# DFT by mirror symmetry in an FNet and MLP block: folded inputs, half the outputs multiplied, and the old program behind a branch

## The chip, the cores and the metric

The kernel runs on one core of one Trainium2 chip. The metric is the device time of one execution in microseconds (us). Engines: TensorE (PE in the profile; its weight loads are PEld) multiplies matrices into PSUM; VectorE (DVE), ScalarE (ACT) and GpSimd (POOL) work on tiles; SyncE (SP) and GpSimd issue the DMAs. Each engine runs its instructions in order, and so does each of the two queues that issue DMAs.

## The reference

One block with two residual branches, each behind a layer norm that a conditioning vector modulates. All tensors are float32; S = 2048 tokens, D = 1024 channels, F = 3584 hidden units.

```python
mod = (silu(c) @ w_mod).reshape(1, 6, 1, -1)
sa, ca, ga, sb, cb, gb = (mod[:, i] for i in range(6))
h = layernorm(x) * (1 + ca) + sa
a = einsum("bsd,ed->bse", h, dft_hid_re);  b = einsum("bsd,ed->bse", h, dft_hid_im)
x = x + ga * (einsum("ts,bse->bte", dft_seq_re, a) - einsum("ts,bse->bte", dft_seq_im, b))
h = layernorm(layernorm(x) * (1 + cb) + sb)
x = x + gb * (gelu(h @ w1 + b1) @ w2 + b2)
```

The four DFT matrices are inputs of the kernel: `dft_seq_re[t, s]` = cos(-2 pi t s / 2048), `dft_seq_im` the sine, and `dft_hid_*` the same with 1024. Nothing in the call says that they are DFT matrices; a kernel that uses their symmetries has to establish them from the numbers.

## The kernel before

**Products.** TensorE works on float16. Each float32 operand is split into a high half and a low half (`hi` on ScalarE, a copy to float16; `lo` on VectorE, the difference), and three of the four half products are summed: `PASSES = ((0, 0), (0, 1), (1, 0))`. A matmul has 128 x 128 weights and 512 moving columns. Where it can, the kernel uses a scheme of seven products for a 2 x 2 block product; `m` in 0 to 6 is the product, and `ORDER = (0, 1, 2, 4, 3, 6, 5)` the order in which they run. The sums and differences that it needs are `comb` on VectorE (L422), the splits L397 on ScalarE and L407 or L409 on VectorE.

**Stages.** The opening loads `wm` and x, makes the rows sa and ca (L485, L507 on TensorE, L493 on VectorE) and normalises x into `hq`. Meanwhile `idle_pe` (L501) runs matmuls whose result nobody reads. `plain1` (L1137) is the sequence DFT of the first 512 output tokens, `winograd1` (L1187) that of the other 1536, `gemm2` (L1423) the hidden DFT of eight blocks of 256 tokens, each followed on VectorE and ScalarE by the second norm (`ln_tasks`) and turned by TensorE (L1321). The other modulation rows (`row_tasks`) and the splits of the hidden DFT matrices and of the first weights lie under these matmuls. Then the MLP: `gemm3(g)` (L1636) is the first layer, 84 matmuls for 256 hidden units and 1024 tokens, and `gemm4(v)` (L1745) the second, 168 matmuls for one pair of g. The tokens go through in two halves, so there are 28 gemm3 and 14 gemm4, in this order: gemm3(0), gemm3(1), gemm3(2), gemm4(0), gemm3(3), gemm3(4), gemm4(1) and so on. In the first half (v = 0 to 6) the weights are split as they come and stored to DRAM; in the second half they are loaded split.

**Order.** Every operation is a task with an engine, an assumed cost and keys that it waits for; a recording layer (`pick`, `fill_to`, `push`) goes through assumed clocks and emits the task that can start first, with a due time as the tie break. The order that it finds is the order in the queues; nothing is reordered on the chip but by waits.

```python
for m in ORDER:                                        # gemm4, one slot for each m
    part(blk, m, ps[b], (0, 1))                        # 12 matmuls, L1745
    after_pe("dve", 1.2, lambda: dve.scalar_tensor_tensor(dst, ps[b], inv, dst, ...), kp[b])   # L1791
```

The eviction of one slot (L1791, 128 x 1024 out of PSUM) has to be through before the same two banks are written again, which in `ORDER` is one slot later for most m.

Of the kernel before, what the change touches and what calls it, by code (L numbers as in the profile page):

```python
# [9 lines left out]
F32 = mybir.dt.float32  # L10
F16 = mybir.dt.float16
I32 = mybir.dt.int32
AF = mybir.ActivationFunctionType
ALU = mybir.AluOpType
RED = bass_isa.ReduceOp
AX = mybir.AxisListType

P = 128
S = 2048
D = 1024  # L20
F = 3584
NS = S // P
ND = D // P
TB = 512
NTB = S // TB
EPS = 1e-5
# [3 lines left out]
SC = 16.0  # L30
SD = 16.0
SZ = 256.0


@with_exitstack
def kernel(ctx, tc, x, cre, cim, dre, dim, w1, b1, w2, b2, c, wm, out):

# [9 lines left out]
    nc = tc.nc  # L49
    pe, act, dve, gp, sp = nc.tensor, nc.scalar, nc.vector, nc.gpsimd, nc.sync  # L50

    pool = ctx.enter_context(tc.tile_pool(name="main", bufs=1))
    psum = ctx.enter_context(tc.tile_pool(name="ps", bufs=1, space=bass.MemoryType.PSUM))
    dram = ctx.enter_context(tc.tile_pool(name="dram", bufs=1, space=bass.MemoryType.DRAM))
    ctx.enter_context(tc.manual_schedule())

    cnt = [0]
# [5 lines left out]
    arena = mk([P, 220 * 256], F32, "arena")  # L63
# [7 lines left out]
    banks8 = psum.tile([P, 8 * 512], F32, tag="ps", name="ps")  # L71
    turn = [0]
    stage = [0]
    held = set()
# [74 lines left out]
    ga_t, sb_t, cb_t, gbb_t = (at(o, 1024) for o in O_ROWS)  # L149


    O_ZC = dict(zip((0, 1, 2, 4, 3, 6, 5), (96, 104, 112, 120, 80, 88, 128)))
    R1 = (136, 138, 140, 142, 216, 218)
    O_K, O_ACC, O_HID = 32, 48, 172
# [4 lines left out]
    w1c = at(0, 14336, F16).rearrange("p (m s a x) -> p m s a x", m=7, s=2, a=2)  # L159
    w2c = at(144, 14336, F16).rearrange("p (m s a x) -> p m s a x", m=7, s=2, a=2)  # L160
    hidc = at(O_HID, 14336, F16).rearrange("p (s m a x) -> p s m a x", s=2, m=7, a=2)
    acc = at(O_ACC, 8192).rearrange("p (b j r e) -> p b j r e", b=2, j=2, r=2)
# [11 lines left out]
    def quad(g):  # L174
        return at(200 + 8 * (g % 2), 2048).rearrange("p (n x) -> p n x", n=4)

    gb2_t = at(28, 1024)

    zc_d = [
        [dram.tile([P, 2, 4, 4, P], F16, tag=f"zc_{h}_{m}", name=f"zc_{h}_{m}") for m in range(7)] for h in range(2)  # L180
    ]
# [8 lines left out]
    row_d = {n: dram.tile([P, D], F32, tag=f"row_{n}", name=f"row_{n}") for n in ("ga", "sb", "cb", "gbb", "gb")}  # L190
    w1_d = [dram.tile([P, 7, 2, 512], F16, tag=f"w1_{g}", name=f"w1_{g}") for g in range(14)]
    w2_d = [dram.tile([P, 7, 2, 2, 512], F16, tag=f"w2_{v}", name=f"w2_{v}") for v in range(7)]
    ident = mk([P, P], F32, "ident")
# [16 lines left out]
    LAT = 0.15  # L210
    GUARD = 0.1
    in_order = [True]
    BEHIND = 0.3

    LAGS = {"w": 2.0, "rowl": 1.0, "crawl": 0.5, "row": 0.2, "z": 1.0, "s": 0.5, "u": 0.3, "op": 0.4, "comb": 0.3, "ln": 0.2}

    LANDS = {"dma": 2.0, "st": 4.0, ("st", "d"): 7.0, ("st", "u"): 5.0, ("st", "s"): 4.0, ("st", "z"): 4.0}
    PE1 = 0.2146
    PE12 = 12 * PE1
    bw = [0.0]  # L220
    clk = {"pe": 0.0, "dve": 0.0, "act": 0.0, "pool": 0.0, "dma": 0.0}
    done = {}
    streams = {}
    ids = [0]
# [154 lines left out]
    ORDER = (0, 1, 2, 4, 3, 6, 5)  # L379


    PLACE = (1, 2, 0, 3)
# [82 lines left out]
    scol, cc = mk([P, ND], F32, "scol"), mk([P, ND], F32, "cc")  # L465
    m1 = mk([P, 6], F32, "m1")
    srep = at(216, 1024).rearrange("p (k m) -> p k m", k=ND)
    mrow, ones = at(O_AUX, 1024), at(O_SO[0], 512)
    sas, ca1s = (at(o, 1024) for o in O_ROW)

    macc, mx = at(O_OP + 16, 2048), mk([P, 5], F32, "mx")
# [129 lines left out]
    xst = [mk([P, 2, 12], F32, f"xst{n}") for n in range(2)]  # L601
# [1386 lines left out]
    flush()  # L1988


# [1 line left out]
def _layout(inputs):  # L1992
    import numpy as np
# [41 lines left out]
```

## Time and profile before

| | |
|---|---|
| median of 3 runs | 1966.1 us (1965.88 to 1969.97) |
| span of the profiled execution | 1964.8 us |
| TensorE busy | 1951.9 us, 99%, granted clock 1.000 |
| VectorE, ScalarE, GpSimd busy | 1423.4, 851.1, 192.0 us |
| DFT stages (L1137, L1187, L1423) | 48.8 to 939.2 us |
| MLP (L1636, L1745) | 939.2 to 1964.8 us |
| DMA | 402 MB, mean 205 GB/s |

How to read it: the page is one profiled execution, which has a span (first to last instruction) and no time of its own beside it; the runs' median is 1.3 us longer. A row of a group has line, engine, operation, out and in, shapes and count, then busy us and mean ns of one, then the idle time before and what ended it. A row of the chain has start, length and what the chain runs through; matmuls of float32 show as two records. A row of stages has the stretch, its length, and each engine's busy time and count, then the granted clock, the DMA share and GB/s.

### The profile page before, as it was taken

Reading aid. Unit: us, or ns where it says so; the run is one execution under the profiler, and the core shown is the slowest. Engines: PE = TensorE matmul, PEld = TensorE weight load, DVE = VectorE, ACT = ScalarE, POOL = GpSimd, SP = SyncE. Lnnn points to the kernel's source line nnn. Section 1 sums busy time; section 2 is a strip of 40 time slices with the busy share of each in tenths; the row PEclk is TensorE's granted clock in tenths of the full one; section 3 lists DMA queues with packets and bytes.
Section 4 is the critical chain, followed back from the end, with each engine's and each line's share of the span. In section 5 each row is a group of like instructions: output and inputs, shape, how many; then the busy total and the mean of one; then the engine's idle time right before and its main releaser. Section 6 shows DMA issues by size and latency. Waiting matters only on the chain.

```text
span 1964.8 us, 23652 instructions
## 1 busy us (share of the span) xinstructions
PE 1951.9 (99%) x9040; PEld 890.0 (45%) x9040; DVE 1423.4 (72%) x1800; ACT 851.1 (43%) x1091; POOL 192.0 (10%) x287
## 2 busy tenths in 40 slices
PE   8999999999999999999999999999999999999999
PEld 3444444444444444444444444444444444444444
DVE  6977886997884477786688998999873453554567
ACT  4843332444542255645577556556323412312311
POOL 0012121221210012212020000000000000000000
PEclk9999999999999999999999999999999999999999
DMA  9258587698588867878855455345476432432324
GB/s 384 76 182 279 171 297 271 236 331 307 215 300 354 327 221 263 280 247 316 327 177 188 150 182 177 134 150 191 177 219 185 129 102 70 134 102 66 113 76 86
DMA packets 139362, 402.41 MB, mean 205 GB/s; under 512 B 15536, under 2 KB 15536, under 8 KB 134640
## 3 DMA queue, kind: packets, MB, share of 16 engines
q1 hardware_dynamic: 111808, 307.30, 46.3%
q0 software_dynamic: 27440, 93.60, 13.3%
q8 instruction: 70, 1.15, 0.2%
q14 instruction: 44, 0.36, 0.1%
HBM read 262.95 MB, written 137.89 MB: 204 GB/s over the span
## 4 chain that ended last, share of the span: by engine, by line
PE 97%; DVE 1%; DMA 1%; issue 1%; POOL 0%; ACT 0%; SPq 0%; POOLq 0%; ACTq 0%; DVEq 0%
PE ps L1636 26%; PE ps L1745 25%; PE ps L1187 22%; PE ps L1423 15%; PE ps L1137 8%; PE ps L1321 1%; PE ps L485 1%; DMA zc<-arena 0%; DMA arena<-in_wm_dram 0%; POOL zc L1357 0%; PE ps L507 0%; DVE arena L655 0%; PE ps L501 0%; PE ps L1497 0%; DVE arena L1791 0%
## 5 line engine op out<-in xcount | busy, mean ns | idle before, releaser
L1745 PE MATMUL ps<-arena 128*128 128x512 f16 x2352 | 510.5, 379 | 3.1 <-ACT arena L1781 3.1
L1636 PE MATMUL ps<-arena 128*128 128x512 f16 x2352 | 510.2, 379 | 0.0
L1187 PE MATMUL ps<-arena 128*128 128x512 f16 x2016 | 435.3, 379 | 0.0
L1745 PEld LDWEIGHTS <-arena 128*128 128x128 f16 x2352 | 230.1, 98 | 281.2 <-issue 4.2
L1636 PEld LDWEIGHTS <-arena 128*128 128x128 f16 x2352 | 230.1, 98 | 276.8
L1791 DVE SCALAR_TENSOR_TENSOR arena<-ps,i4c,arena 128x1024 f32<-128x1024 f32 x179 | 229.4, 1282 | 145.9 <-PE ps L1745 144.2
L1187 PEld LDWEIGHTS <-arena 128*128 128x128 f16 x2016 | 197.3, 98 | 237.9
L1423 PE MATMUL ps<-arena 128*128 128x512 f16 x1344 | 292.2, 379 | 0.0
L397 ACT ACTIVATE arena<-arena,shc 128x512 f16<-128x512 f32 (+1 forms) x115 | 116.0, 1018 | 277.9 <-PE ps L1745 181.4
L1423 PEld LDWEIGHTS <-arena 128*128 128x128 f16 x1344 | 131.5, 98 | 155.9
L422 DVE TENSOR_TENSOR arena<-arena 128x512 f32<-128x512 f32 (+1 forms) x228 | 171.4, 754 | 4.6 <-ACT arena L1655 0.3
L1137 PE MATMUL ps<-arena 128*128 128x512 f16 x768 | 166.5, 379 | 3.7 <-ACT arena L539 2.1
L703 ACT ACTIVATE arena<-arena 128x1024 f16<-128x1024 f32 x100 | 103.5, 1050 | 144.2 <-PE ps L1187 86.1
L409 DVE SCALAR_TENSOR_TENSOR arena<-arena,shc 128x512 f16<-128x512 f32 (+1 forms) x115 | 128.7, 1122 | 34.7 <-ACT arena L397 34.5
L706 DVE SCALAR_TENSOR_TENSOR arena<-arena 128x1024 f16<-128x1024 f32 x100 | 132.9, 1349 | 20.2 <-ACT arena L703 20.2
L1662 DVE TENSOR_TENSOR arena<-arena,ps 128x512 f32<-128x512 f32 x84 | 57.6, 686 | 113.4 <-PE ps L1636 110.0
L1655 ACT ACTIVATE arena<-arena,b1s,i1c 128x512 f32<-128x512 f32 x84 | 68.3, 813 | 139.1 <-DVE arena L1662 139.0
L1137 PEld LDWEIGHTS <-arena 128*128 128x128 f16 x768 | 74.8, 98 | 95.4 <-ACT arena L539 2.6
L798 DVE TENSOR_TENSOR arena<-arena 128x1024 f16<-128x1024 f32 x56 | 67.3, 1219 | 20.3 <-ACT arena L795 20.2
L397 ACT ACTIVATE arena<-arena,s1c 128x512 f16<-128x512 f32 (+1 forms) x70 | 60.5, 884 | 47.2 <-DVE arena L422 24.4
L795 ACT ACTIVATE arena<-arena 128x1024 f16<-128x1024 f32 x56 | 57.7, 1047 | 51.4 <-DMA u<-arena 36.4
L1658 ACT ACTIVATE arena<-ps 128x512 f32<-128x512 f32 x84 | 49.8, 593 | 54.5 <-PE ps L1636 54.3
(169 smaller groups left out, 1413.0 us busy)
## 6 DMA issues: line engine op xcount, KB each, us to landing
w<-arena SPq DMA_DIRECT2D x64, 512.0 KB, 4.7
arena<-w SPq DMA_DIRECT2D x119, 256.0 KB, 2.7
u<-arena POOLq DMA_DIRECT2D x56, 512.0 KB, 6.7
arena<-u SPq DMA_DIRECT2D x112, 256.0 KB, 4.1
arena<-w SPq DMA_DIRECT2D x56, 512.0 KB, 3.6
arena<-s SPq DMA_DIRECT2D x48, 512.0 KB, 6.6
arena<-in_cre_dram SPq DMA_DIRECT2D x32, 512.0 KB, 7.2
arena<-in_cim_dram SPq DMA_DIRECT2D x32, 512.0 KB, 6.0
```

Source lines behind the costliest of these rows:

```text
L397: act.activation(o[m][0], q(j), AF.Copy, **sc)
L409: dve.scalar_tensor_tensor(o[m][1], q(j), scale, o[m][0], op0=ALU.mult, op1=ALU.subtract)
L422: dve.tensor_tensor(q(d), q(a), q(b), op=op)
L703: h = Task("act", 1.15, lambda: act.activation(o[:, :, 0], s2, AF.Copy, scale=SC), list(deps) + free)
L706: dve.scalar_tensor_tensor(o[:, :, 1], s2, SC, o[:, :, 0], op0=ALU.mult, op1=ALU.subtract)
L1137: pe.matmul(bank_of(d_), hleft(d_, s, kp, a), cop(n)[:, s, b], start=(kp == 0 and s == 0 and a == 0 and b == 0), stop=(kp == 7 and s == 1 ...
L1187: pe.matmul(bank_of(st + ch), left, cop(n)[:, s, b], start=(start and kp == 0 and s == 0 and a == 0 and b == 0), stop=(kp == 3 and s == 1 ...
L1423: pe.matmul(bank_of(bk), up(N)[:, c_, a], dp(n)[:, c_, w], start=(start and ri == 0 and c_ == 0 and i == 0), stop=(ri == 1 and c_ == 3 and ...
L1636: pe.matmul(ps.rearrange("p (k t) -> p k t", k=4), w1c[:, m, s, a, d * P : (d + 1) * P], zc(m)[:, b, :, d, :], start=(start and d == 0 and ...
L1655: act.activation(dst, src, AF.Gelu_apprx_tanh, scale=inv, bias=b1s[:, 2 * p + j : 2 * p + j + 1])
L1745: pe.matmul(t[:, j], hidc[:, c_, m, a, k * P : (k + 1) * P], w2c[:, m, c_, w], start=(start and c_ == 0 and n == 0), stop=(c_ == 1 and n = ...
L1791: lambda: dve.scalar_tensor_tensor(dst, ps[b], inv, dst, op0=ALU.mult, op1=ALU.add), kp[b],
```

## The change

The old function is renamed `general` and otherwise left as it is. A new function `fast` stands ahead of it:

- **Folds.** For a DFT of length N, cos at N - s equals cos at s and sin has the other sign, and at N/2 - s the sign alternates with the output's parity. `fast` normalises x, transposes it (`ln1`), applies the modulation per channel in the transposed layout, and adds and subtracts mirror images in both dimensions (`folds`; rows that are their own mirror go through `special`). The folded inputs are a quarter as long in each dimension and come in even and odd kinds.
- **Half the outputs.** `hid_unit` multiplies 18 pieces with 513 columns, `seq_tile` 16 tiles of 128 tokens; the other half of the channels of each tile is the same two products with the other sign (`low`, `up`), and the tiles of mirrored tokens use negated operands (`neg_tasks`).
- **Rows.** `row` makes ga, cb, sb and gb with TensorE in float32, each from eight 512 KB loads through three buffers.
- **Second norm** (`ln2`), transposes (`turn`) and `z_tasks` follow per block of 256 tokens as before; the four blocks of the first half leave their splits where the MLP reads them. `b2 * gb` is added to the output by 16 accumulating DMAs when the MLP starts.
- **MLP.** `gemm3` and `gemm4` are those of before. The splits of the first two w1 groups stand in the front, those of w1 group 2 and w2 pair 0 now behind the start of the MLP.
- **Checks.** From gemm4(6) on, `chk_tasks` reads the four matrices again from DRAM, 148 units of up to 128 x 512: each loads a piece and its mirror image (40 of them by an index list), subtracts or adds on VectorE and sums squares on ScalarE, through three pairs of buffers. `verdict` adds up; if the sum is above 2 to the power -60, the branch runs `general`, which computes and overwrites everything.
- The filler matmuls of `idle_pe` are not in `fast`.

```diff
-def tile_fnet_mlp_kernel(ctx, tc, x, cre, cim, dre, dim, w1, b1, w2, b2, c, wm, out):
+def general(ctx, tc, x, cre, cim, dre, dim, w1, b1, w2, b2, c, wm, out):
...
+def fast(ctx, tc, x, cre, cim, dre, dim, w1, b1, w2, b2, c, wm, out):
...
+                def fold(e=e, o=o, bd=bd, pos=pos, neg=neg):
+                    dve.scalar_tensor_tensor(o, bank(bd), neg, e, op0=ALU.mult, op1=ALU.add)
+                    dve.scalar_tensor_tensor(e, bank(bd), pos, e, op0=ALU.mult, op1=ALU.add)
...
+    def folds(cls):
...
+        def s1(arr, op):
+            o = FA(eo(0, arr, cls, 0), (4 * AR, 2), (AR, 2), (1, 512))
+            dve.tensor_tensor(o, o, FA(eo(0, arr, cls, m), (4 * AR, 2), (AR, 2), (-1, 512)), op=op)
...
+    def cop_item(t, ch):
+        q, c_ = divmod(ch, 2)
+        def f(o):
+            for hf in range(2):
+                sp.dma_start(
+                    FA(o, (512, 2), (1, 512), p0=64 * hf, pn=64),
+                    cri[t][0:2, q::2, 2 * c_ + hf, :].rearrange("b p t -> p b t"),
+                )
+        def use(o, key, last):
+            src = FA(o, (1, 2), (2, 512))
...
+            split("cop", src, hi, lo, SC, [key], last, 1024, 42.0 + ch)
...
+    def row(n, j):
+        for k in range(ND):
+            m = ND * n + k
+            o = WRING[m % 3]
+            l = load(("wr", m), lambda o=o, k=k, j=j: sp.dma_start(FA(o, (1, 1024)), wm[:, k, j * D : (j + 1) * D]),
+                [("wru", m - 3)] if m > 2 else [("tpd", 3), ("n", 15)], stream="ld")
+            def f(k=k, o=o):
+                for h in range(2):
+                    pe.matmul(bank(6 + h), scol[:, k : k + 1].to_broadcast([P, P]), FA(o + 512 * h, (1, 512)),
+                        start=k == 0, stop=k == 7)
...
+    def hid_unit(tp, t, cls, c_):
...
+            for par, pm_, o, w in ((0, ev, 255, 257), (1, od, 512, 256)):
+                mm_ = [
+                    (HA(hop(cls, loc, a, j, t, pm_, u0), (1, m)), HA(dop(t, b, j, 257 * par), (1, w)))
+                    for j in range(2) for a, b in PASSES
+                ]
...
+    def seq_tile(i):
...
+            mm_ += [
+                (HA(cop(tp, 1, a, ch, kk), (1, 128)), HA(aop(tp, 1, b, ch), (257, 2), (1, 256)))
+                for ch in range(4) for a, b in PASSES
+            ]
...
+        def low():
+            dve.tensor_tensor(
+                FA(y, (1, 2), (2, 256)), PA(pb + 255, (257, 2), (1, 256)), qv(i, 0, (257, 2), (1, 256)), op=ALU.subtract)
+        def up():
+            dve.tensor_tensor(
+                FA(y + 512, (1, 2), (2, 256)), PA(pb + 511, (256, 2), (-1, 256)), qv(i, 256, (256, 2), (-1, 256)), op=ALU.add)
...
+    def chk_unit(load_a, load_b, diffs, sq, pn=P):
+        n = chks[0]
+        chks[0] += 1
+        ka, kb_ = CB[n % 3]
+        a, b = at(ka, 512), at(kb_, 512)
+        free = [("chk", n - 3)] if n > 2 else []
+        deps = [add("chkl", "st", 0.0, lambda: load_a(a), free, ("chka", n))]
...
+        for cost, f in diffs:
+            k = add("chkd", "dve", cost, lambda f=f: f(a, b), deps if k is None else [k], None, 1e7)
+        f = lambda: act.activation(sq(a), sq(a), AF.Square, accum_out=csum[0:pn, n : n + 1])
+        add("chks", "act", 0.7, f, [k] if k else deps, ("chk", n), 1e7)
...
+    def parity(even):
+        def f(o, op):
+            def g(a, b):
+                dve.tensor_tensor(a[:, o::2], a[:, o::2], b[:, o::2], op=op)
+            return g
+        return [(0.4, f(0, ALU.subtract if even > 0 else ALU.add)), (0.4, f(1, ALU.add if even > 0 else ALU.subtract))]
...
+    def gather(mat, idx, col_):
...
+            gp.indirect_dma_start(
+                out=b, out_offset=None, in_=rows_, in_offset=bass.IndirectOffsetOnAxis(ap=idx[:, col_ : col_ + 1], axis=0))
...
+    def plain(v, pn=P):
+        return lambda t: gp.dma_start(t[0:pn], v)
...
+    def verdict():
+        v = csum[:, 0:1]
+        dve.tensor_reduce(v, csum, axis=AX.X, op=ALU.add)
+        gp.partition_all_reduce(v, v, P, RED.add)
+        dve.tensor_scalar(v, v, 2.0**-60, None, op0=ALU.is_le)
+        dve.tensor_scalar(v, v, -1.0, 1.0, op0=ALU.mult, op1=ALU.add)
+        dve.tensor_copy(odd_i, v)
...
+    for i in range(NS):
+        f = lambda i=i: gp.dma_start(o_s[i // 8, i % 8], gbb_t, accum_op=ALU.add)
...
+            if v == 6:
...
+                chk_tasks()
+                n = chks[0]
+                add("chkd", "dve", 2.0, verdict, [("chk", n - 1 - j) for j in range(3)], "verdict", 1e7)
+    flush()
+    return nc.values_load(odd_i[0:1, 0:1])
...
+def tile_fnet_mlp_kernel(tc, *args):
+    odd = fast(tc, *args)
+    with tc.If(odd > 0):
+        general(tc, *args)
```

1371 lines of the change are left out of this document (1370 added, 1 removed).

## The prediction

> **What bounds the kernel now.** I read the page's busy shares, then the chain of work that ended last in order of time, then three stretches of the table by stage.
>
> ```profile
> PE 1951.9 (99%) x9040; PEld 890.0 (45%) x9040; DVE 1423.4 (72%) x1800; ACT 851.1 (43%) x1091; POOL 192.0 (10%) x287
> ```
> ```profile
> 48.82 153.85 PE ps L1137 x712
> 202.66 435.12 PE ps L1187 x2016
> ...
> 917.62 20.72 PE ps L1423 x96
> ...
> 939.22 18.13 PE ps L1636 x84
> ...
> 976.35 1.75 PE ps L1321 x16
> ...
> 1936.03 24.78 PE ps L1745 x114
> ```
> ```profile
> 0.00:42.00 42.00, 36.46 (x107) 14.20 (x108) 25.07 (x46) 16.22 (x26) 1.58 (x6) 1.00 0.97 380
> ...
> 1083.00:1156.00 73.00, 73.00 (x340) 33.07 (x339) 67.69 (x104) 43.45 (x59) 2.43 (x4) 1.00 0.53 180
> ...
> 1523.00:1596.00 73.00, 73.00 (x340) 33.09 (x339) 30.36 (x32) 23.47 (x27) 0.00 (x0) 1.00 0.36 101
> ```
> TensorE is the bound from 49 us to the end. A matmul of 512 float16 columns costs 18.13/84 = 0.2158 us, so 256 columns cost 0.108. The DFTs (L1137, L1187, L1423) fill the time to 939 us, the MLP the 1026 us behind. In the MLP's first half VectorE is busy 67.69 of 73 us behind TensorE, in the second only 30.36.
>
> **What goes.** The three DFT groups have 768 + 2016 + 1344 = 4128 matmuls, 891 us. In the built order of the changed program their place is taken by 297 matmuls of at most 257 columns (hidden DFT) and 200 of 512 and 400 of 257 or 256 columns (sequence DFT): 43 + 75 = 118 us. So TensorE no longer bounds the front; VectorE and the hand-offs do. I therefore add up VectorE's front in its built order, with these durations:
>
> ```profile
> L422 DVE TENSOR_TENSOR arena<-arena 128x512 f32<-128x512 f32 x200 | 137.3, 688 | 4.2 <-ACT arena L1655 0.3
> L422 DVE TENSOR_TENSOR arena<-arena 128x1024 f32<-128x1024 f32 x28 | 34.2, 1221 | 0.4
> L409 DVE SCALAR_TENSOR_TENSOR arena<-arena,s1c 128x512 f16<-128x512 f32 x42 | 31.0, 746 | 6.5 <-ACT arena L397 6.4
> L409 DVE SCALAR_TENSOR_TENSOR arena<-arena,s2c 128x1024 f16<-128x1024 f32 x49 | 61.8, 1279 | 3.8 <-ACT arena L397 3.8
> L493 DVE SCALAR_TENSOR_TENSOR arena<-arena,scol 128x2048 f32<-128x2048 f32 x2 | 4.7, 2352 | 3.8 <-DMA arena<-in_wm_dram 3.8
> L614 DVE BATCH_NORM_STATS2 xst<-arena 128x6 f32<-128x512 f32 x4 | 2.5, 669 | 0.0
> L1251 DVE TENSOR_TENSOR lns<-lns 128x2 f32<-128x2 f32 x14 | 2.3, 161 | 0.5
> L397 ACT ACTIVATE arena<-arena 128x512 f16<-128x512 f32 x56 | 32.7, 619 | 14.2 <-DVE arena L422 13.8
> L1304 ACT ACTIVATE arena<-arena,lns 128x1024 f32<-128x1024 f32 x16 | 19.0, 1231 | 9.2 <-DVE lns L1301 9.1
> ```
> The new reversed and two-step accesses appear in no row; I price them by element count. From below they cost that, from above double, and some 60 instructions of the front have one: 0 to 60 us. I take 0, since an element costs VectorE 1.2 to 1.5 ns in these rows whatever the operands are.
>
> **A, to the first fold: 55 us.**
> ```profile
> 15.06 3.43 PE ps L485 x8
> ...
> 27.09 3.66 PE ps L507 x8
> ```
> ```profile
> 1.48 5.14 PE L501 MATMUL ps<-arena 128*128 128x512 f16 x12 [1.48 <-DVE mx L1463]
> ...
> 18.33 1.89 PE L501 MATMUL ps<-arena 128*128 128x512 f16 x8
> ```
> Four float32 matmuls (eight records) cost 3.43. L507 starts when the last modulation weights land, behind 9 MiB; now four x tiles stand ahead instead of two, so 1 MiB more at 380 GB/s, 2.8 us: 29.8. Two groups of four follow: 37, or 40 with a TensorE that ran cold, as the first twelve above did (0.43 us each against 0.24). Maximum, row copies, 18 one-column matmuls and scaling I estimate at 7: 47. Eight statistics and small steps precede the first fold in VectorE's order: 8.
>
> **B, folds: 68 us, to 123.** 26 STT of 512 (19.4), 6 TT of 2048 (13.7), 4 STT and 4 TT of 1024 (10.0), the rest statistics and small (14.7): 57.8. For normalising, turning and activating the third and fourth batch behind ScalarE I add 10.
>
> **C, hidden DFT: 107 us, to 230.** Here TensorE's order decides. The four modulation rows are now made by TensorE, 32 steps of two float32 matmuls (1.71 us), placed between the hidden DFT's matmuls as 51, then 14 steps, 15, 2 steps, 54, 8 steps, 45, 8 steps, 132. Whatever stands behind a step waits for its 512 KB load.
> ```profile
> arena<-in_wm_dram SPq DMA_DIRECT2D x32, 512.0 KB, 6.9
> ...
> zc<-arena POOLq DMA_DIRECT2D x56, 256.0 KB, 4.7
> ...
> w<-arena POOLq DMA_DIRECT2D x9, 256.0 KB, 3.5
> ...
> row_ga<-arena POOLq DMA_DIRECT2D x1, 512.0 KB, 2.9
> ```
> SP reaches these loads only when the fifth sequence-DFT piece has freed its buffer (eight STT, one split: 7.3 us), and they land 4 later: 11.5. Three buffers turn in 1.71 + 0.4 + landing; landing 2.9 to 6.9 gives 1.7 to 3.0 us a step. I take 2.0, nearer the short row, as little else is moving. 14 steps 28, then 1.7 + 3.4 + 5.9 + 15.1 + 4.9 + 15.1 + 14.3 (the first three steps of each group have landed): 88.4. Sum 100; bounds 93 and 128. VectorE has only 49 us of work here. The first sequence tile adds 5.4 and its copies: 7.5.
>
> **D, sequence DFT and second norm: 226 us, to 456.** VectorE: 113 TT of 512 (77.6), 52 STT of 1024 (69.3), 16 TT of 1024 (19.5), 6 STT of 512 (4.5), 134 small (21.7): 192.6. ScalarE has 78 copies of 512 (48) and 80 squares and passes of 1024 (some 95), TensorE about 6.3 us a tile against VectorE's 12; both lie beside it. Idle I estimate at 28 (10 while two tiles fill the pipe, 8 in the last norm's hand-offs, 10 between), bounds 8 and 60. Two activations, a copy and 16 transposes (1.75) follow before the MLP starts: 5.2.
>
> **E, MLP: 1032 us.** 4704 matmuls, 1015.3. At its start VectorE still has 15 TT (10.3) and 46.6 us of weight and hidden splits before the first second-layer eviction, against 54.4 us of TensorE; ScalarE has eight copies and two squares ahead of the first eviction. Before, these splits lay under the DFT. Estimate 17, bounds 5 and 40.
>
> **F, checks under the MLP: 10 us.** The 148 units, each of which loads a piece of a DFT matrix and its mirror image, subtracts and squares, stand from the seventh pair of layers on: 133 before the last eviction, about 22 in each 73 us. Their VectorE work, 0.8 us, fits the 43 idle; but VectorE waits in order for GpSimd's loads, and the evictions queue behind it.
> ```profile
> L1025 POOL DMA_DIRECT2D w<-arena x15 | 8.3, 551 | 52.7 <-DVE arena L409 33.4 <-DVE lns L1240 6.0 <-ACT arena L1304 4.6
> L1819 POOL DMA_DIRECT2D out_dram<-arena x4 | 4.8, 1197 | 467.0 <-DVE arena L1791 467.0
> L929 POOL PARTITION_ALL_REDUCE sums<-sums x21 | 11.9, 566 | 381.6 <-DVE sums L925 379.6 <-DVE sums L933 2.0
> ```
> A buffer's turn is VectorE 0.8, ScalarE 0.8, two issues of 0.55, landing 3.5 to 4.7, signals 0.4: 6.6 to 7.8, against three eviction slots of 2.59 = 7.8. It just fits. 40 units gather by index, for which no row exists: from the 0.55 of a plain issue (nothing) to the 1.2 of an accumulating one plus a landing late by half a slot, 1.5 us each (60). I take 10, near the plain issue.
>
> **G, behind the last eviction: 37 us.** 15 units still stand there, with nothing beside them. Three have landed (2.4); twelve more take four turns of 7.3, less 2 for two that only square: 27; the verdict 3.3 (reduction over partitions 0.57, five small steps, signals); register loads and the branch 4, in no row, from 2 to 10. Bounds 27 and 52. It cannot be nothing: the units are in the order. The Trainium skill (DMA: Bandwidth & Descriptors, "Anatomy of one DMA — SWDGE (gpsimd) path") gives 2.0 us plus bytes at 436 GB/s, 2.6 us for 256 KB, where this trace has 3.5 and 4.7; by it the tail would be about 5 us shorter, an estimate.
>
> **Sum.** 55 + 68 + 107 + 226 = 456; + 1032 + 10 + 37 + 2 for the last evictions = 1537 of span; the span before was 1964.8 beside a median of 1966.1, so 1.3 around it: 1538 us.
>
> **Rivals.** *Better overlap:* C 7 less, D's idle at 8, E at 5, G at 27: 1489. For it: VectorE's 67.69 of 73. Against: there the order had slack, here it alternates with ScalarE.
>
> *Checks stall the evictions:* F at 60, G at 52, because gathers are slow: 1603. For it: a turn of 7.8 has no slack. Against: the low DMA share there.
>
> *Cold TensorE:* without the filler matmuls of L501, its work in C (about 83 us) and D runs at half speed, as in the twelve above. C then takes 11.5 + 32 x 3.42 + 53 = 174 (+74), D some 15 more: 1627. Against: in C TensorE is asked for nearly without pause. By the Trainium skill (TensorE: Matmul & The Clock Gate, "Part 1: The HAM clock gate (the 'warmup' mystery)") a window of about 3.4 us without work sets the clock to half. The trace's start at 0.43 us agrees; no long pause follows in it to show a fall.
>
> *The verdict goes the other way (slower):* the sum of squared deviations must stay below 2 to the power -60 = 8.7e-19; above it, the old program runs as well, 1538 + 1965 = 3503. It decides at one value off by 1e-9. The inputs, computed as the reference computes them, deviate by at most 1.5e-12 between mirror images, squares summing to some 4e-21. That leaves only an arithmetic surprise on the chip.
>
> **How the numbers follow.** Forecast 0.60, better overlap 0.12, stalling checks 0.12, cold TensorE 0.12, both programs 0.04. From 1470 (better overlap, and VectorE a little quicker) to 1630 (the cold case and part of the strided accesses). A difference of 0.2% (4 us) is about what a measurement can tell from no change: faster 0.95, same 0.01, slower 0.04.
>
> **What would show it.** In the profile after: first fold near 55, hidden DFT ending near 222, first MLP matmul near 456, TensorE solid from there to about 1500, and VectorE, ScalarE and GpSimd alternating for 37 us without TensorE. A first MLP matmul outside 410 to 520, holes in the second half's matmuls, or any line of the old program would prove the sum wrong.

## The result, and the profile after

The changed kernel takes 1565.2 us (median of 4 runs, 1560.4 to 1573.3) against 1967.2 us for the kernel before beside it: a ratio of 0.796 (95% interval 0.794 to 0.799). Forecast were 1538 us, with a range of 1470 to 1630. The profiled execution took 1573.3 us with a span of 1571.5, so it is one of the longer ones; two experiments below have the same front and reached the MLP 4 to 5 us sooner, which is how far single times of the front can be trusted.

From the page: the busy shares, and the granted clock in 40 slices.

```profile
PE 1319.7 (84%) x6081; PEld 635.8 (40%) x6081; DVE 1121.2 (71%) x1723; ACT 738.6 (47%) x1173; POOL 254.4 (16%) x415
...
PEclk9555999968658999999999999989999999999995
```

TensorE lost 632 of its 1952 us, the kernel 393 of its span. The difference is TensorE's idle time: 252 us, where there were 13. No line of the old program ran. The table by stage (columns: stretch, its length, then busy time and instructions of PE, PEld, DVE, ACT, POOL, granted clock, DMA share, GB/s) shows where it idles:

```profile
0.00:55.00 55.00, 36.32 (x113) 21.37 (x113) 35.18 (x78) 21.39 (x38) 6.54 (x20) 0.84 0.76 297
55.00:146.00 91.00, 24.80 (x123) 19.63 (x124) 67.79 (x92) 43.24 (x63) 0.65 (x1) 0.58 0.27 71
146.00:265.00 119.00, 109.24 (x452) 52.35 (x451) 32.80 (x36) 21.03 (x27) 1.61 (x4) 0.93 0.56 188
265.00:469.00 204.00, 117.31 (x693) 78.72 (x692) 177.63 (x359) 129.27 (x203) 23.97 (x39) 0.74 0.40 139
469.00:585.00 116.00, 101.63 (x423) 43.57 (x421) 74.71 (x126) 70.05 (x94) 20.38 (x28) 0.89 0.77 205
585.00:1020.00 435.00, 435.00 (x2017) 197.25 (x2016) 384.07 (x510) 230.62 (x298) 13.07 (x18) 1.00 0.51 175
1020.00:1120.00 100.00, 88.62 (x398) 39.34 (x397) 48.05 (x86) 45.96 (x85) 34.56 (x65) 0.95 0.87 289
1120.00:1428.00 308.00, 308.00 (x1429) 139.62 (x1428) 207.87 (x308) 133.80 (x265) 102.31 (x165) 1.00 0.70 235
1428.00:1533.00 105.00, 98.78 (x446) 43.90 (x444) 82.09 (x103) 33.16 (x71) 37.04 (x54) 0.97 0.61 185
1533.00:1571.00 38.00, 0.00 (x0) 0.00 (x0) 11.04 (x31) 10.04 (x30) 14.30 (x23) 0.54 0.48 162
```

The first stretch ends at the first fold, the second with the folds, the third with the hidden DFT, the fourth with the sequence DFT and second norm. Then come the MLP's start, its solid middle, the checks' start, and the rest. In the second stretch TensorE works a quarter of the time at 0.58 of its clock, and the DMA engines move 71 GB/s: nothing is full there. In the fourth VectorE is busy 178 of 204 us. The timeline of TensorE has the seams (start, length, line, count, and in brackets the idle time before with what ended it):

```profile
145.58 9.92 PE L2874 MATMUL ps<-arena 128*128 128x256 f16 x42 [13.55 <-ACT arena L2659]
...
241.16 17.09 PE L2874 MATMUL ps<-arena 128*128 128x257 f16 x132
...
551.49 33.48 PE L3547 MATMUL ps<-arena 128*128 128x512 f16 x144 [4.47 <-ACT arena L3583]
...
1052.44 15.76 PE L3438 MATMUL ps<-arena 128*128 128x512 f16 x60 [9.03 <-ACT arena L3460]
...
1527.94 4.88 PE L3547 MATMUL ps<-arena 128*128 128x512 f16 x12 [4.54 <-DVE arena L3593]
```

The hidden DFT begins in earnest at 145.58 and ends at 258.25, the first MLP matmul stands at 469.02, the last ends at 1532.82.

New accesses, grouped by form: the folds with a reversed operand (L2690, L2696), a normalising pass read forward and reversed (L2603, L2604), and the checks' half-row differences, gathers and plain loads (columns: count, busy us, mean ns, idle before).

```profile
L2696 DVE TENSOR_TENSOR arena<-arena 128x2048 f32<-128x2048 f32 x4 | 9.2, 2291 | 0.1
L2690 DVE TENSOR_TENSOR arena<-arena 128x2048 f32<-128x2048 f32 x4 | 9.2, 2288 | 0.0
...
L2604 ACT ACTIVATE arena<-arena,lnc 128x512 f32<-128x512 f32 x12 | 9.6, 802 | 0.0
L2603 ACT ACTIVATE arena<-arena,lnc 128x512 f32<-128x512 f32 x12 | 9.6, 801 | 0.7 <-DVE lnc L2594 0.7
...
L3352 DVE TENSOR_TENSOR arena<-arena 128x256 f32<-128x256 f32 x240 | 92.3, 422 | 73.0 <-DMA arena<-in_cre_dram 38.6 <-DMA arena<-in_dim_dram 12.0 <-DMA arena<-in_cim_dram,idxs 9.2
...
L3369 POOL DMA_DIRECT2D arena<-in_cre_dram x99 | 54.3, 548 | 126.0 <-ACT arena L3345 117.5 <-issue 6.5 <-DMA arena<-fw 0.4
...
L3362 POOL DMA_INDIRECT arena<-in_cre_dram,idxs x16 | 17.0, 1063 | 4.9 <-issue 4.9
```

2048 reversed elements cost VectorE 2.29 us, where 2048 straight ones cost 2.35 before, in another operation. Like with like, `up` (L2974), which reads in reverse and writes every second element, takes 683 ns for 512 elements, and a straight TENSOR_TENSOR (L2365) 688. ScalarE pays the same forward and backward. So the strided accesses cost nothing extra, as taken. VectorE idled 73 us before the checks' differences, for loads; most of that is its own slack, and TensorE lost 17 us in holes after 1020.

### The profile page after: what moved, and what is told of

Its sections match the earlier page's. It is cut to its first block, busy times and chain, and to the rows that moved or that the text cites. A ratio compares the mean times of both kernels' runs of the same rounds, so it can differ in the third digit from the quotient of the medians.

```text
span 1571.5 us, 17349 instructions
## 1 busy us (share of the span) xinstructions
PE 1319.7 (84%) x6081; PEld 635.8 (40%) x6081; DVE 1121.2 (71%) x1723; ACT 738.6 (47%) x1173; POOL 254.4 (16%) x415
## 4 chain that ended last, share of the span: by engine, by line
PE 66%; DVE 12%; DMA 9%; issue 7%; ACT 3%; POOL 2%; SPq 1%; DVEq 0%; POOLq 0%; ACTq 0%
PE ps L3438 28%; PE ps L3547 27%; PE ps L2818 3%; DMA arena<-in_wm_dram 3%; PE ps L2874 3%; DMA arena<-in_cre_dram 2%; PE ps L2947 2%; PE ps L2959 1%; DMA arena<-in_w_dram 1%; PE ps L2500 1%; DVE arena L2365 1%; DVE arena L2350 1%; DVE arena L2352 1%; DMA arena<-in_dim_dram 1%; DMA arena<-in_cim_dram,idxs 1%
## 5 line engine op out<-in xcount | busy, mean ns | idle before, releaser
L3438 PE MATMUL ps<-arena 128*128 128x512 f16 x2352 | 521.3, 384 | 19.5 <-ACT arena L3460 16.7
L3547 PE MATMUL ps<-arena 128*128 128x512 f16 x2352 | 515.2, 381 | 12.3 <-DVE arena L3593 7.7
L3438 PEld LDWEIGHTS <-arena 128*128 128x128 f16 x2352 | 232.7, 99 | 305.7 <-issue 35.0
L3547 PEld LDWEIGHTS <-arena 128*128 128x128 f16 x2352 | 231.2, 98 | 294.0 <-issue 19.6
L3345 ACT ACTIVATE arena<-arena 128x512 f32<-128x512 f32 (+5 forms) x148 | 91.5, 619 | 191.1 <-DVE arena L3352 125.1
L2365 DVE TENSOR_TENSOR arena<-arena 128x512 f32<-128x512 f32 (+1 forms) x228 | 171.5, 754 | 5.8 <-ACT arena L3067 1.1
L3352 DVE TENSOR_TENSOR arena<-arena 128x256 f32<-128x256 f32 x240 | 92.3, 422 | 73.0 <-DMA arena<-in_cre_dram 38.6
L2947 PE MATMUL ps<-arena 128*128 128x256 f16 (+3 forms) x400 | 55.9, 304 | 29.7 <-DVE arena L2974 29.5
L3164 POOL PARTITION_ALL_REDUCE sums<-sums x21 | 12.8, 609 | 402.8 <-DVE sums L3160 398.0
L3369 POOL DMA_DIRECT2D arena<-in_cim_dram x99 | 54.2, 548 | 135.6 <-ACT arena L3345 133.2
L3369 POOL DMA_DIRECT2D arena<-in_cre_dram x99 | 54.3, 548 | 126.0 <-ACT arena L3345 117.5
L2619 PE MATMUL ps<-ident,arena 128*128 128x128 f32 x128 | 26.5, 378 | 53.7 <-ACT arena L2603 52.6
L2352 DVE SCALAR_TENSOR_TENSOR arena<-arena,s1c 128x512 f16<-128x512 f32 (+1 forms) x70 | 66.3, 958 | 7.1 <-ACT arena L2340 7.1
L3063 PE MATMUL ps<-ident,arena 128*128 128x128 f32 x128 | 24.7, 357 | 54.4 <-ACT arena L3053 42.8
L2818 PE MATMUL ps<-arena,scol 128*128 128x512 f32 x128 | 63.4, 640 | 8.3 <-DMA arena<-in_wm_dram 7.1
```

The source lines that it names most:

```text
L2352: dve.scalar_tensor_tensor(o[m][1], q(j), scale, o[m][0], op0=ALU.mult, op1=ALU.subtract)
L2365: dve.tensor_tensor(q(d), q(a), q(b), op=op)
L2818: pe.matmul(bank(6 + h), scol[:, k : k + 1].to_broadcast([P, P]), FA(o + 512 * h, (1, 512)), start=k == 0, stop=k == 7,)
L2947: pe.matmul(PA(pb + o, (1, w)), l, r, start=n == 0, stop=n == len(mm_) - 1)
L3345: f = lambda: act.activation(sq(a), sq(a), AF.Square, accum_out=csum[0:pn, n : n + 1])
L3352: dve.tensor_tensor(a[:, o::2], a[:, o::2], b[:, o::2], op=op)
```

## The experiments

Five things were to be settled: what made the folds late, what the low clock cost, what bounds the sequence DFT's stage, what the checks cost, and whether the findings make a faster kernel. Each was timed beside the kernel before, whose medians lay between 1966.8 and 1967.4 us.

### Loads ahead of the fold

In the changed kernel, SyncE loaded no piece of the sequence matrix between 64 and 109 us, and ScalarE's split of one stood in front of the fourth batch's normalising:

```profile
62.77 1.24 SPq L2763 DMA_DIRECT2D arena<-in_cim_dram  x2
109.01 1.25 SPq L2763 DMA_DIRECT2D arena<-in_cre_dram  x2
...
116.16 1.11 ACT L2475 ACTIVATE arena<-arena 128x1024 f16<-128x1024 f32 x1 [7.97 <-DMA arena<-in_cim_dram]
...
118.03 0.48 PE L2619 MATMUL ps<-ident,arena 128*128 128x128 f32 x1 [35.19 <-ACT arena L2603]
```

The pieces turn in three buffers. A buffer comes free with VectorE's share of the split, which stood behind the folds and the fourth batch's statistics; so the loads behind it were late, and ScalarE waited for them in order.

```
-            split("cop", src, hi, lo, SC, [key], last, 1024, 42.0 + ch)   # due time
+            split("cop", src, hi, lo, SC, [key], last, 1024, 63.0 + ch)
-    for ch in range(4): for t in range(2): cop_item(t, ch)               # eight, ahead of the rows
+    the first three here, the other five between the row loads: one for every third
```
(The splits of the one-row pieces also got an earlier due time, 20 instead of 41, and a stream of their own in the planner.)

> The splits of the sequence-DFT matrix pieces (ScalarE's copy and VectorE's difference) are placed behind the normalising of the fourth batch of rows instead of between the batches, and the last five of the eight piece loads stand between the row loads in SyncE's queue instead of ahead of them. Theory (the pieces held up step B): in the changed kernel ScalarE waited 8.0 and 8.2 us for two of these loads, and TensorE 35 and 13.6 us behind it; without that the hidden DFT should begin near 120 us instead of 145.6, with up to 10 us given back between the row steps: 1540 us (1530 to 1552). Rival (SyncE's queue is the bound either way, and the five pieces only push the row loads back): no gain, 1560 to 1572.

Measured: 1556.3 us (1554.9 to 1557.6), 9 less than the changed kernel's median.

```profile
110.40 0.81 ACT L2603 ACTIVATE arena<-arena,lnc 128x512 f32<-128x512 f32 x1 [3.01 <-DVE lnc L2594]
...
164.08 6.88 PE L2819 MATMUL ps<-arena,scol 128*128 128x512 f32 x12 [4.31 <-DMA arena<-in_wm_dram]
...
226.63 14.69 PE L2877 MATMUL ps<-arena 128*128 128x257 f16 x114
```

The mechanism is there, but the gain is a third of the 25 us expected, and between the two expectations. The fourth batch is normalised 7 us sooner, without a wait for a load, and the hidden DFT ends at 241.3 instead of 258.2. But the work behind the fourth batch (row steps, here) starts at 129, where 120 was expected: the batch now waits for VectorE's statistics (3.01 above), which stand behind the folds. The rival's price is small: TensorE waits 10 us between the first row step and the last hidden-DFT matmul (4.31 the longest wait), in the changed kernel 8. The first MLP matmul came at 452.1 us. Four later kernels that keep this edit have it at 449.0 to 456.8, three without it (further down, one of them with fillers) at 463.4 to 465.0: some 11 us at that point between the means, of which 9 are left at the end.

### The low clock

Filler matmuls keep TensorE busy where it idled.

```
                 def turn(g=g, j=j, bk=bk):
+                    if bt == 2 and g == 0 and j == 0:
+                        140 matmuls of 512 float16 columns of `ones` into bank(bk)
...
+                if n == 0 and par == 1:          # first unit of the hidden DFT
+                    50 such matmuls into bank(4)
```

> 190 filler matmuls of 512 float16 columns on a constant tile are added to TensorE in the front: 140 ahead of the transposes of the third batch (where it idled 35 us) and 50 inside the first unit of the hidden DFT (where it idled 13.6 us). Nothing else moves. Theory (the low granted clock cost little, since TensorE is not the bound there): what was slow on the path are 42 hidden-DFT matmuls (9.9 us against about 5.3) and four row steps (9.4 against 7.3): a gain of 4 to 9 us, 1559 us. Rival (cold TensorE as priced in the prediction, 74 us in the hidden DFT and 15 behind it): a gain of over 40 us, below 1525. Other rival (the fillers end too late and stand in the way): 1570 or more.

Measured: 1587.6 us (1583.2 to 1592.5), 22 slower, as the second rival had it. The fillers stood one batch too early; batches count from 0, and the long hole is before batch 3:

```profile
68.50 30.38 PE L2621 MATMUL ps<-arena 128*128 128x512 f16 x140 [0.42 <-ACT arena L2663]
98.72 3.66 PE L2623 MATMUL ps<-ident,arena 128*128 128x128 f32 x32
```

The third batch's transposes, due at 72, came at 98.7. That says nothing about the clock. The second try changes `bt == 2` to `bt == 3`.

> The same 190 filler matmuls as in the run before, but the first 140 one batch later: ahead of the transposes of the fourth batch, where TensorE really idled for 35 us (82.8 to 118.0 us of the changed kernel). In the earlier run they stood ahead of the third batch's transposes, which were needed at 72 us, so they were late by 26 us. Theory (the low clock in front costs little): the 42 hidden-DFT matmuls take 5.5 instead of 9.9 us, the first row steps 1.8 instead of 2.35 each: 5 to 8 us less, 1558 us. Rival (cold TensorE, 89 us as priced in the prediction): below 1525. If nothing else hangs on it: 1565.

Measured: 1568.5 us (1566.4 to 1571.7): no gain, where 5 to 8 us were expected.

```profile
86.45 30.38 PE L2621 MATMUL ps<-arena 128*128 128x512 f16 x140
...
148.72 5.51 PE L2882 MATMUL ps<-arena 128*128 128x256 f16 x42 [2.76 <-ACT arena L2663]
```

The 42 matmuls do run warm, 5.51 us instead of 9.92, and the hidden DFT ends some 5 us sooner (253.4, against 256.5 to 260.0 in six profiles without fillers). By the first MLP matmul it is gone: 463.4 us, against 463.9 and 465.0. Where in between it went was not followed further.

### What bounds the sequence DFT's stage

Three kernels change TensorE's work there, the first two that alone. The first doubles it:

```
-                for n, (l, r) in enumerate(mm_):
+                for n, (l, r) in enumerate(2 * mm_):
+                    n %= len(mm_)                # start again in the same bank
```

> Every accumulation group of the sequence DFT is multiplied twice, the second time starting anew in the same bank, so that the result stays; TensorE gets about 87 us more work (16 tiles of 12 matmuls of 0.216 us and 26 of 0.11 us), no other engine any. Theory (VectorE bounds this stage, TensorE lies beside it): 5 to 25 us slower, 1570 to 1590. Rival (TensorE, or the hand-offs to and from it, bound the stage): 60 to 87 us slower, 1625 to 1652.

The second keeps one pass of three (`PASSES[:1]` in both groups):

> The sequence DFT multiplies one of its three passes (high by high) and leaves out the two that carry the low halves; the result is coarser, nothing else moves, and the order of the instructions is that of the changed kernel. TensorE's work in this stage falls from 87 to about 31 us. Doubling that work cost 79 us; this asks whether the stage as it stands is bound by TensorE's turn in the chain. Theory (VectorE bounds the stage in its fixed order, which only has no slack for a later TensorE): VectorE waited 7.9 us for these matmuls, so 5 to 15 us less: 1555 us. Rival (the engines alternate, and TensorE's turn counts at nearly its whole length): 40 us less, 1525.

The third is the first with the planner told of it (`2.7` to `5.4`, `2.75` to `5.5`):

> The sequence DFT multiplied twice as in the earlier run, but the planner that writes the order of instructions is told of it (5.4 and 5.5 us instead of 2.7 and 2.75 for the two groups of a tile), so that the other engines' work is put around the longer groups. Theory (the stage is VectorE's, and the earlier 79 us came because the fixed order had VectorE wait for a later TensorE): 174 us of TensorE beside 178 of VectorE should overlap in part: 25 to 50 us slower than the changed kernel, about 1605. Rival (tiles pass from engine to engine with only two in flight, so TensorE's turn counts whatever the order): 1640 again.

Measured: 1644.5 us (1642.9 to 1647.6) twice, 1555.5 (1550.3 to 1556.3) with one pass, 1628.2 (1626.4 to 1631.6) twice and planned for. What VectorE waited for in this stage (total us, times, longest), in the changed kernel, and then with the doubled work:

```profile
DVE lns L3023 <- ACT lns L3022: 9.4, 5, 3.8
DVE arena L2969 <- PE ps L2947: 7.9, 3, 5.8
```
```profile
DVE arena L2971 <- PE ps L2948: 31.7, 7, 11.3
DVE lns L3025 <- ACT lns L3024: 25.0, 7, 8.7
```

The first came out where its rival had it (1625 to 1652), 79 us slower; the second where its theory had it. From the hidden DFT's last matmul to the first MLP matmul there are 206.3 and 206.9 us in two kernels that leave this stage alone (210.8 in the changed kernel's own profile), with TensorE busy for 119 to 123 of them. With a third of the passes it is busy for 72 and the stage takes 194.6: some 48 us less of TensorE bring 12. Doubled it is busy for 205 and the stage takes 277.7, so some 85 us more cost 67 to 71; planned for, 262.9, or 52 to 57. VectorE is busy for 178 to 182 us of this stretch in all of them. So as it stands the stage is in the main VectorE's, and TensorE's matmuls lie beside it, as the prediction had it. But they lie there with hardly any slack. Two tiles are in flight and VectorE takes them in order; with the doubled work its waits for TensorE grow from 7.9 to 31.7 us, and those for ScalarE's root from 9.4 to 25.0. A new plan recovers 15 of the 70 us. The third kernel came out between its two expectations and nearer the rival: planning brought 16 us of the 40 that I had hoped for.

### The checks

Left out altogether, with the verdict and the branch:

```
-                chk_start()
-                chk_tasks()
...
-                add("chkd", "dve", 2.0, verdict, ...)
-    with tc.If(odd > 0):
-        general(tc, *args)
```

> The 148 check units, the verdict and the branch to the old program are left out; the program always takes the folded way. Theory (steps F and G): 13 to 16 us of holes in the second half's matmuls and all but about 4 us (the last output write) of the 38.7 us behind the last matmul go: 1565 less 48, 1517 us (1512 to 1522). Rival (the holes come from the weight loads themselves, with the checks as bystanders): only the tail goes, 1530.

Measured: 1506.3 us (1505.2 to 1509.1), below the expected range. The checks cost 59 us, not 48. The second half's holes go, and 4.4 us remain behind the last matmul. From the end of pair 0 on the two profiles differ by 57 us: 17 of holes, 34 behind the last matmul, and the rest in the main in cold matmuls behind the holes; the expectation had counted the holes up to 1463 alone.

```profile
1464.01 36.66 PE L3547 MATMUL ps<-arena 128*128 128x512 f16 x168
```

Then the same checks, handed over earlier:

```
             gemm3(g, {13: reload, 27: lasts}.get(g))
+            if g == 13:
+                chk_start(); chk_tasks(); ...     # was behind gemm4 of pair 6
```

> The check units are handed to the order of work after the first layer of group 13 instead of behind the second layer of pair 6, 54 us of TensorE earlier; nothing else is changed. Theory (the end is 15 units that had no cover, at 7.3 us for each three): most of the 15 move ahead of the last eviction, 20 to 30 us less at the end, against at most 5 us of new stalls: 1541 us (1535 to 1550). Rival (VectorE is over 85% busy with the weight and hidden splits in that stretch, so the check work delays evictions by as much as it saves): 1560 to 1570.

Measured: 1548.4 us (1545.3 to 1554.6), 17 less. Behind the last matmul are left 10 us instead of 38.7, but some 9 us of new holes and cold matmuls stand before, one of them just ahead of the last 36 matmuls:

```profile
1523.53 9.87 PE L3547 MATMUL ps<-arena 128*128 128x512 f16 x36 [7.05 <-DVE arena L3593]
```

### Together, and what stood in the way next

> The pieces of the sequence-DFT matrix later (9 us less by itself) and the check units 54 us of TensorE earlier (17 us less by itself), together. They act at opposite ends of the kernel. Theory (the gains add): 1539 us (1533 to 1545). Rival (the earlier front only lets the weight loads of the MLP's start be waited for longer): 1548, as with the checks alone.

Measured: 1539.4 us (1533.6 to 1542.0). The gains add, 26 = 9 + 17. TensorE's longest hole in the second half is now one of 8.3 us at 1035. In the first 60 us of the checks GpSimd's queue carries something else as well, and the loads stand behind it in the queue (what TensorE waited for, the timeline of GpSimd, then the DMA issues from 960 to 1110: count, KB each, median us to landing):

```profile
PE ps L3441 <- DVE arena L3467: 8.3, 1, 8.3
```
```profile
988.44 2.69 POOL L3648 DMA_DIRECT2D out_dram<-arena  x3 [2.70 <-DVE arena L3596]
...
1005.05 1.12 POOL L3372 DMA_DIRECT2D arena<-in_cre_dram  x2 [4.09 <-issue]
```
```profile
arena<-in_cre_dram POOLq DMA_DIRECT2D x64, 256.0 KB, 4.6
...
out_dram<-arena POOLq DMA_DIRECT2D x8, 512.0 KB, 10.3
...
arena<-in_cre_dram,idxs POOLq DMA_INDIRECT x6, 5.4
```

So the planner was told to reckon 8 us, not 2.8, for the loads of the first 16 units:

> As the kernel with both moves, but the planner reckons 8 us instead of 2.8 from issue to landing for the first 16 check units, since in the first 60 us of the checks GpSimd's queue also carries eight accumulating writes of 512 KB that took 10.3 us each to land, and VectorE waited there up to 14.5 us for one check load. Theory (the holes at the checks' start are late loads): 6 to 12 us less than with both moves, 1530 (1527 to 1534). Rival (the evictions are late there for the copies out of the second matmul layer, whatever the checks do): 1539.

Measured: 1532.2 us (1529.0 to 1533.7), 7 less by the medians and in the range expected. The two profiles show only half of that in the checks. The hole of 8.3 us is gone, but 16 us instead of 10 stand behind the last matmul, and from the end of pair 0 to the end of the span there are 962.5 us instead of 966.1. The rest lies in the front, which this edit leaves alone: it reached the MLP 7.8 us sooner in this profile. So some 4 of the 7 us are shown to come from the slack. Next the MLP's start, where the DMA engines are full and weight loads late, with 11.1 us to landing against a median of 4.0 over the whole kernel (the changed kernel, DMA issues from 470 to 560):

```profile
out_dram<-arena POOLq DMA_DIRECT2D x16, 512.0 KB
...
arena<-in_w_dram SPq DMA_DIRECT2D x4, 256.0 KB, 11.1
```
```
-    for i in range(NS): push("gbb", "gbb", [Task("pool", 1.5, f)], 1e6)   # at the MLP's start
+    ... pushed behind gemm4 of pair 0
```

> As the run before, and the sixteen accumulating writes that add the last bias to the output (512 KB each on GpSimd's queue, at 479 to 545 us of the changed kernel, where the DMA engines were over 90% busy) are handed over after the second layer of pair 0 instead of at the MLP's start. Theory (the weight loads at the MLP's start, 11.1 us to landing instead of 4.0, were late for these writes): the start stall of 25 us falls to about 15: 8 to 10 us less, 1521 (1516 to 1527). Rival (the stall is the splits' own chain between ScalarE and VectorE): 1530.

Measured: 1541.2 us (1533.4 to 1547.5), 9 slower, which neither expectation had. Nearly half of the start's stall goes (from the first MLP matmul to the end of pair 0 it is 14 us of stall instead of 25; the 5 and 14 that the next expectation names leave out the first two waits), but the block of writes makes a hole one pair later, with another for 3.7 us right behind it:

```profile
601.54 4.42 PE L3442 MATMUL ps<-arena 128*128 128x512 f16 x12 [11.30 <-ACT arena L3464]
```

Spread instead, one write behind slots 0, 2 and 4 of each block in the second layers of pairs 0, 1 and 2:

> As the kernel with both moves and the slack for the first check units, but the sixteen accumulating writes of the last bias are spread: one behind every second or third step of the second layers of pairs 0, 1 and 2, some 6 us apart, with none at the MLP's start. Handed over in one block after pair 0 they took the start stall from 14 to 5 us but made a new hole of 18 us at 590 to 610. Theory (each block of these writes fills the DMA engines and makes the next weight loads late; spread, 512 KB at a time fits beside them): the start stall stays at 5 us and the hole goes: 1523 us (1519 to 1527). Rival (weight loads wait for any such write): some of the hole stays, 1530 or more.

Measured: 1521.6 us (1520.7 to 1525.3), a ratio of 0.773 (0.772 to 0.774): the fastest here with the checks in, 44 us under the changed kernel. The start's stall stays at 14 us, and where the hole was, 1.71 us are left:

```profile
590.33 5.34 PE L3442 MATMUL ps<-arena 128*128 128x512 f16 x24 [1.71 <-ACT arena L3464]
```

## Why the prediction was right, and where it was not

The whole came out 27 us above the forecast, inside the range; by its points the changed kernel's profile stands against it like this. Of the three signs that were to prove the sum wrong, one appeared: the second half's matmuls have five holes, 17 us together, where F had priced 10. The hidden DFT ended at 258, not near 222; the first MLP matmul, at 469, lies inside 410 to 520.

**What goes.** Right. TensorE stops bounding the front, and the MLP is solid from 585 to 1020 at 0.2158 us a matmul.

**A, 55 us.** 56.0. Right.

**B, to 123.** The hidden DFT starts in earnest at 145.6: the term that failed, 22 us short. VectorE's work was priced at 57.8 and was 67.8 in that stretch; three piece splits (1.22 us each) and two folds of the second half (2.29 each) that I had put under C ran here, in the waits. The 10 us for "normalising, turning and activating" became 23 of idle. I had listed which queue waits for the piece buffers, but put that wait, 11.5 us, at the start of C behind SyncE's queue; it fell in B, on ScalarE, whose order holds both splits and normalising. The pieces-later run shows it: with those splits moved, the work behind the fourth batch starts at 129, near the 123 forecast, and the first MLP matmul comes some 11 us sooner.

**C, 107 us.** From 145.6 to the first eviction of a sequence tile at 265.4 there are 120. The 11.5 us of waiting at the start were not there; instead 42 matmuls ran cold (9.9 us). The row steps took 71 us, not 61.6: a step cost 2.0 to 2.3 us in the groups of 8 and 14, nearly as taken, but the group of two took 7.2 with its waits for loads, forecast 3.4. And the hidden DFT's matmuls were dearer than 0.108 us: 17.09 for the last 132, forecast 14.3. What makes them so is in the last section.

**D, 226 us.** 203.6 from that eviction to the first MLP matmul at 469.0, so 22 too much, which hid B's miss. The instructions were counted well: the durations of VectorE's rows there sum to 195.7 us, forecast 192.6. But neighbours overlap, and it was busy 177.6. Idle was 26, the hand-off to the MLP among it, where 28 and 5.2 were forecast. That VectorE bounds the stage held for the kernel as it is; "lies beside it" did not mean spare.

**E, start stall 17.** The 420 matmuls up to 585.0 take 116 us instead of 90.6: 25, within 5 to 40. I looked for the stall in the splits. With the sixteen accumulating writes moved away, in the last two runs, it is 14; in the eleven profiled kernels that have them here it is 21 to 27. So some 7 to 12 us of it hang on those writes, most likely by the weight loads that were late beside them. What makes the other 14 was not tested.

**F, 10 us.** The holes from 1020 to 1463 sum to 12.8, with some 3 us of low clock behind them: 16. "It just fits" was right after the start. At the start it did not fit: there the queue carries accumulating writes too, and slack for the loads removed the hole of 8.3 us in the kernel with both moves. Gathers cost 1.06 us to issue against 0.55, and landed in 5.4 against 4.6 (in the kernel with both moves): within the price given.

**G, 37 us.** 37.9 behind the last eviction, at 1533.6, and right in its parts:

```profile
1562.97 0.32 DVE L3429 TENSOR_REDUCE csum<-csum 128x1 f32<-128x160 f32 x1 [0.84 <-ACT arena L3345]
...
1564.74 0.15 DVE L3433 CAST oddi<-csum 128x1 int32<-128x1 f32 x1
```

The units end at 1562.9, 29.3 us (2.4 + 27 forecast); the verdict takes 2 (3.3), what follows 6.6 (4, from 2 to 10). Before it, the last evictions cost 7 instead of 2: a hole of 4.5 and twelve cold matmuls. The 2.6 us for 256 KB, an estimate from the Trainium skill (DMA: Bandwidth & Descriptors, "Anatomy of one DMA — SWDGE (gpsimd) path"), are not met here: loads land in 4.6 under traffic (the kernel with both moves), and in the quiet tail the chain of waits of the changed kernel (start, length) has them at

```profile
1536.04 3.67 DMA arena<-in_dim_dram
...
1556.34 4.20 DMA arena<-in_dim_dram
```

so the rows of the trace before, 3.5 and 4.7, though of writes to DRAM, were the better price.

**Sum.** +1, +22, +13, -22, +8, +6 and +6 make 34: 1537 of span became 1571 in this profile. Two misses of 22 us cancelled, so the total is better than its parts.

**Rivals.** *Cold TensorE*, 89 us: the fall of the clock is real: 0.58 granted in the stretch with long pauses, 0.24 us a matmul where warm ones cost 0.13. The Trainium skill's rule (TensorE: Matmul & The Clock Gate, "Part 1: The HAM clock gate (the 'warmup' mystery)") agrees with it. The rival's price was wrong by far. C's steps are asked for without long pauses, as the prediction said against it (0.93 granted), and warming the hole brought 5 us that were gone by the end of D. D itself was never warmed (0.74 granted). The run with one pass speaks against a high price there: it takes 48 us of TensorE's time out of D, at a clock still lower, for a gain of 12. *Stalling checks* happened in small; the checks' whole price, measured by leaving them out, is 59 us against 47 forecast. *Better overlap* and *both programs* did not occur.

## What to carry to other kernels

When a change frees the bounding engine, price the new front by its queues: for each in-order engine ask which loads its instructions wait for, and who must free the buffer behind that load. Work that hides under another engine is not free if the plan leaves it no slack: two thirds of TensorE's passes taken out moved that stage by about a quarter of the time that they took, all of them added once more by four fifths. And before moving a block of transfers, look at who shares its queue and the DMA engines at the place it goes to; spreading it gained what moving it in one piece lost.

## What the runs showed of the hardware

Neighbours on VectorE overlap in the profile: the durations of the 359 instructions in the 204 us of the fourth stretch sum to 195.7 us, and they were busy 177.6. In 218 cases an instruction starts before the one ahead has ended, mostly by 0.07 to 0.09 us. A sum of durations is about 10% too long there, and 7% over the whole kernel (1202.8 against 1121.2).

A matmul with four rows is not cheaper than one with 128, and going from 128 rows to four and back costs extra. Units of the hidden DFT have twelve full matmuls of 256 or 257 columns and one or two groups of three with four rows; ScalarE's evictions show their cadence:

```profile
247.91 0.60 ACT L2475 ACTIVATE arena<-ps 128x513 f16<-128x513 f32 x1 [1.26 <-PE ps L2874]
249.77 0.60 ACT L2475 ACTIVATE arena<-ps 128x513 f16<-128x513 f32 x1 [1.26 <-PE ps L2874]
252.17 0.60 ACT L2475 ACTIVATE arena<-ps 128x513 f16<-128x513 f32 x1 [1.80 <-PE ps L2874]
```

Units come 1.86 us apart with one group, and 2.40 with two: 0.54 for a group. The starts of the single matmuls in the trace say where it goes. Full ones start mostly 0.11 us after each other. The first one with four rows starts 0.20 us after the full one ahead of it, the next two 0.12 and 0.11 after that, and the full one behind them 0.20 after the last. So it is the two changes that cost, some 0.09 us each. The last 132 matmuls hold twelve such groups, 2.2 us of the 2.8 over the forecast. Between 128 and 65 rows, in the sequence DFT, the starts show no such step: 0.11 us into and out of the matmul with 65. What makes the changes cost was not looked for.
